# PSUM handed out by single banks and later by pairs, with the second layer's output products in another order

## The chip, the cores and the metric

The kernel runs on one core of one Trainium2 chip. The metric is the device time of one execution in microseconds. TensorE (PE in the views; its weight loads are PEld) multiplies matrices into PSUM, which has eight banks of 512 fp32 columns on 128 partitions. VectorE (DVE) and ScalarE (ACT) read PSUM and work on SBUF, GpSimd (POOL) works on SBUF, and SyncE (SP) issues all transfers.

## What is computed

Causal attention over 32 heads of 576 tokens with a bias from a running sum, and then two dense layers with nonlinearities, 2304 tokens wide, in fp32:

```python
s_pos = np.maximum(s, 0.0)
cum = np.cumsum(s_pos, axis=-1)
bias = -(cum[:, :, :, None] - cum[:, :, None, :])
scores = np.where(causal, -1000000000.0, scores + np.minimum(bias, 0.0))
attn = np.exp(scores - np.max(scores, axis=-1, keepdims=True))
attn = attn / (np.sum(attn, axis=-1, keepdims=True) + 1e-09)
x = (attn @ v)                       # reordered to 2304 x 512
h = x @ w_in;   x = (h - np.tanh(h)) @ w_out          # layer 1, 512 -> 2048 -> 512
h = x @ w2_in;  x = (h * np.clip(h + 3.0, 0.0, 6.0) / 6.0) @ w2_out    # layer 2
```

## The kernel before

**Precision.** A matrix product with fp32 accuracy is made of three products of rounded halves: high by high, low by high, high by low. So nearly every operand exists as a high and a low part. ACT makes the high part by a copy, DVE (or POOL) the low part by a subtraction.

**Order.** The kernel hands its work to a planner (`Plan`, L134). Every piece of work is an `op` with an engine, an assumed duration, what must come before it, the buffers it takes (`Buf`) and a priority. `schedule` (L163) plays the plan through: an engine that is free takes the ready piece with the lowest priority number for which all buffers are free in their `Pool`. The pieces are then written out in the order of their planned starts. On the chip each engine executes its own list in that order and waits on semaphores where data or a buffer is not free yet. What an instruction waits for is found per tile, so a change of the tiles changes waits even where the lists stay equal.

**PSUM.** Four tiles `wide0` to `wide3` of 1024 columns, two banks each (L287). In attention `wide0` as a whole takes the first part of the row maxima. The six halves of the other three are the pool `banks` (L290). After the last row maximum the halves of `wide0` join it (L706). In layer 1 the hidden results come from the halves of `wide0` and `wide1` (`hidp`), the four accumulators from those of `wide2` and `wide3` (`accp`). In layer 2 a product needs two banks; `Pairs` (L96) hands out the first `wide` tile whose two halves are free.

**Attention** (L424 to L662), for each head: `mx` (L500, TensorE) multiplies queries and keys and `rd` (L509, DVE) takes row maxima from PSUM; `st` (L593) makes scores in four chunks, `ex` (L596, ACT) exponentials into `pt`; `pv` (L624) multiplies `pt` with the values into two banks, and ACT copies them out (L647).

**Layer 1** goes over five token blocks (512, 512, 256, 512, 512) and in each over 16 slices of 128 hidden columns (`step_ops`, L833). A step is: hidden matmuls in three parts of four (L842), tanh on ACT (L853), the subtraction on DVE (L857), a copy on ACT into `gg` (L861), the low half on DVE (first three blocks) or POOL (L863), and output matmuls in three parts of four (L873) into the accumulators. Beside it the weights are unpacked and, in `group` (L937), those of layer 2 are prepared into seven pieces for each quarter and stored in DRAM (`wdram`).

**Layer 2** multiplies 2x2 block matrices with seven products instead of eight. For each of three groups of 768 tokens: `prepare` (L1051) loads the inputs and splits seven operands into `op` tiles (`split_tile`, L1045: ACT L1047, DVE L1048; additions L926). `hidden_group` (L1071) makes the seven hidden products for each of four quarters (12 matmuls of 384 columns each, L1091) with copies and additions on ACT and DVE (L1099, L1102). `out_phase` (L1133) makes the seven output products, each over the four quarters (18 matmuls of 256 columns for each quarter, L1164), with their operand splits, and stores the outputs. The products are named by the numbers in `ORDER` (L54); the position in it sets priorities. Products 1, 6, 7 and 4 add up in one pair of banks (`chain`), 5 and 3 in a second, 2 in a third. Product 4 comes after the result of product 7 is added to `p5` (`c22`), since it goes on adding to the same pair. Operands of the output products use the pool `oop`, three buffers before. Every product has its weight piece of 512 KB loaded from `wdram` (`weights`, L1039) into one of the buffers of `piecep`: the two halves of the layer-1 weight slots 4 to 8, ten in all (L1020).

## Time and profile before

| | |
|---|---|
| median of 3 runs | 1008.09 us (1007.0 to 1009.53) |
| the profiled execution | 1012.46 us, span 1010.7 us |
| mean granted TensorE clock in it | 0.996 |
| TensorE busy | 966.9 us, 96% of the span, 5560 matmuls |
| weight loads, DVE, ACT, POOL busy | 840.2, 660.3, 466.2, 160.7 us |

The views are of the one profiled execution; its span runs from the first to the last instruction. The end of a matmul is modelled and overlaps the next one's start, so matmuls are 0.37 us long in the mean where they start every 0.23 us. A wait is named after what ended it.

### The profile page before, as it was taken

The numbers are of one execution on the slowest core, as the hardware profiler recorded it, in microseconds if no ns is written. First come the engines' busy times: TensorE is split into PE (matmuls) and PEld (weight loads), VectorE is DVE, ScalarE is ACT, GpSimd is POOL, SyncE is SP. The second block draws the span as 40 slices with busy tenths as digits, with TensorE's granted clock in tenths as the row PEclk, the third lists the DMA queues.
The fourth block names the chain that finished last, engine by engine and source line by source line (L and its number), as shares of the span: only waits on it lengthen the run. The fifth ranks groups of instructions, "written<-read, shape, count | busy, mean of one in ns | idle before, by whom it ended". The sixth has DMA issues, their size and how long they took to land.

```text
span 1010.7 us, 15024 instructions
## 1 busy us (share of the span) xinstructions
PE 966.9 (96%) x5560; PEld 840.2 (83%) x5560; DVE 660.3 (65%) x1106; ACT 466.2 (46%) x714; POOL 160.7 (16%) x106
## 2 busy tenths in 40 slices
PE   4989989999999999999999999999899998999998
PEld 3667766767777777898888888899899998999998
DVE  7765665746997766677557674365954659455673
ACT  2556655664543444344434434344544445344442
POOL 8243636440000000001223222100000000000000
PEclk9999999999999999999999999999999999999999
DMA  4644857477633654655454763488788886887872
GB/s 118 173 132 119 209 149 194 143 214 253 205 108 108 227 183 160 239 168 189 186 182 142 250 230 135 145 266 268 257 264 281 251 284 228 273 282 251 251 244 82
DMA packets 71816, 203.24 MB, mean 201 GB/s; under 512 B 11778, under 2 KB 20482, under 8 KB 70464
## 3 DMA queue, kind: packets, MB, share of 16 engines
q1 hardware_dynamic: 71744, 202.29, 63.1%
q8 instruction: 44, 0.72, 0.3%
q14 instruction: 28, 0.23, 0.1%
HBM read 151.09 MB, written 44.09 MB: 193 GB/s over the span
## 4 chain that ended last, share of the span: by engine, by line
PE 83%; DVE 9%; ACT 4%; issue 3%; DMA 1%; POOL 0%; DVEq 0%; ACTq 0%; POOLq 0%
PE wide L842 20%; PE wide L873 18%; PE wide L1091 17%; PE wide L1164 11%; PE wide L624 9%; PE wide L593 6%; DVE junk L509 2%; PE wide L500 2%; ACT pt L596 1%; DVE f_w L926 1%; DVE op_W L1048 1%; DVE op_B L1048 1%; DMA xr<-xdram 1%; DMA f_w<-xdram 1%; DVE g L857 0%
## 5 line engine op out<-in xcount | busy, mean ns | idle before, releaser
L842 PE MATMUL wide<-xx,w 128*128 128x512 f32 (+1 forms) x960 | 235.5, 371 | 3.0 <-DVE g L857 2.9
L873 PE MATMUL wide<-gg,w 128*128 128x512 f32 (+1 forms) x960 | 234.7, 369 | 0.4 <-ACT gg L861 0.3
L842 PEld LDWEIGHTS wide<-xx,w 128*128 128x128 f32 x960 | 168.5, 188 | 39.1 <-DVE g L857 8.4
L873 PEld LDWEIGHTS wide<-gg,w 128*128 128x128 f32 x960 | 170.4, 188 | 31.3 <-ACT gg L861 1.2
L509 DVE CUSTOM_DVE_ANT_0 junk<-wide,maskA 128x384 bf16<-128x384 f32 (+4 forms) x160 | 86.8, 542 | 57.2 <-PE wide L500 28.2
L624 PE MATMUL wide<-pt,vf 128*66 128x320 f32 (+4 forms) x448 | 116.0, 373 | 7.2 <-DVE Mt L509 4.5
L853 ACT ACTIVATE g<-wide 128x512 f32<-128x512 f32 (+1 forms) x80 | 44.4, 555 | 135.7 <-PE wide L842 57.1
L863 POOL TENSOR_TENSOR gg<-g,gg 128x512 fp32r<-128x512 f32 x32 | 48.0, 1501 | 358.4 <-ACT gg L861 268.0
L857 DVE TENSOR_TENSOR g<-wide,g 128x512 f32<-128x512 f32 (+1 forms) x80 | 50.7, 634 | 79.4 <-ACT g L853 60.9
L593 PE MATMUL wide<-Q,K 128*128 128x320 f32 (+9 forms) x384 | 94.4, 367 | 5.9 <-ACT pt L596 3.2
L1164 PE MATMUL wide<-w,op_B 128*128 128x256 f32 x702 | 92.5, 284 | 4.7 <-DVE op_B L1048 4.7
L1164 PE MATMUL wide<-w,op_W 128*128 128x256 f32 x702 | 91.9, 284 | 2.2 <-DVE op_W L1048 1.3
L1164 PEld LDWEIGHTS wide<-w,op_B 128*128 128x128 f32 x702 | 87.7, 191 | 6.1 <-DVE op_B L1048 6.1
L1164 PEld LDWEIGHTS wide<-w,op_W 128*128 128x128 f32 x702 | 87.5, 191 | 3.6 <-DVE op_W L1048 2.1
L596 ACT ACTIVATE pt<-wide 128x512 f32<-128x512 f32 (+2 forms) x128 | 62.4, 501 | 60.5 <-PE wide L593 30.5
L593 PEld LDWEIGHTS wide<-Q,K 128*128 128x128 f32 (+1 forms) x384 | 65.2, 198 | 29.8 <-ACT pt L596 10.6
L1091 PE MATMUL wide<-op_w,w 128*128 128x384 f32 x432 | 80.0, 335 | 0.1
L861 ACT ACTIVATE gg<-g 128x512 fp32r<-128x512 f32 (+1 forms) x80 | 47.0, 587 | 64.8 <-DVE g L857 34.0
L1091 PEld LDWEIGHTS wide<-op_w,w 128*128 128x128 f32 x432 | 75.1, 188 | 0.9 <-DVE g L857 0.6
L624 PEld LDWEIGHTS wide<-pt,vf 128*66 128x66 f32 (+1 forms) x448 | 51.7, 141 | 20.9 <-DVE Mt L509 5.8
L500 PE MATMUL wide<-K,Q 66*128 66x384 f32 (+5 forms) x192 | 48.6, 369 | 15.9 <-DMA K<-rb 9.9
L446 POOL TENSOR_TENSOR Q<-tq,Q 64x1152 fp32r<-64x1152 f32 (+1 forms) x17 | 42.4, 2493 | 79.5 <-PE wide L593 36.4
(261 smaller groups left out, 1274.5 us busy)
## 6 DMA issues: line engine op xcount, KB each, us to landing
w<-wdram SPq DMA_DIRECT2D x168, 512.0 KB
wdram<-cv SPq DMA_DIRECT2D x56, 512.0 KB
raw_c<-in_w_dram SPq DMA_DIRECT2D x11, 1024.0 KB
raw_b<-in_w_dram SPq DMA_DIRECT2D x11, 1024.0 KB
raw_a<-in_w_dram SPq DMA_DIRECT2D x12, 512.0 KB
vf<-in_v_dram SPq DMA_DIRECT2D x16, 330.0 KB
rb<-rdram SPq DMA_DIRECT2D x8, 576.0 KB
xdram<-xb SPq DMA_DIRECT2D x16, 288.0 KB
```

What stands on the lines that cost most here:

```text
L500: nc.tensor.matmul(r(b)[0:rr, col + k0 : col + k0 + n], qa[0:66, i * P : i * P + rr], ka[0:66, k0 : k0 + n], start=True, stop=True,)
L509: nc.vector.tensor_tensor_reduce(out=junk[0:rr, 0:w], in0=r(b)[0:rr, col : col + w], in1=maskA[0:rr, m0 : m0 + w], scale=1.0, scalar=-3.0e ...
L593: nc.tensor.matmul(o, w, x, start=(i == 0), stop=(i == len(mms) - 1))
L596: nc.scalar.activation(r(pt), r(b)[:, 0 : CW[c]], AF.Exp, scale=0.125)
L624: nc.tensor.matmul(r(po[bank])[0:DV, oc : oc + n], r(vf)[0:rr, j, hh, :], r(pts[c])[0:rr, col : col + n], start=(j == 0), stop=(bank == 0 ...
L842: nc.tensor.matmul(r(ps)[:, 0:w], wt[:, c, :], x(c)[:, 0:w], start=(part == 0 and c == 0), stop=(part == 2 and c == NCC - 1),)
L857: nc.vector.tensor_sub(x, r(ps)[:, 0:w], x)
L861: gho = plan.op("ACT", vec_us(w, 1.2, 205), lambda: nc.scalar.activation(r(gh)[:, 0:w], r(g)[:, 0:w], AF.Copy), [m, to_gg], [g, gh], base)
L863: glo = plan.op("DVE" if beside else "POOL", vec_us(w, 0.96, 155) if beside else vec_us(w, 0.44, 160), lambda: (nc.vector if beside else n ...
L873: nc.tensor.matmul(r(acc[e])[:, 0:w], a[:, es], bb[:, 0:w], start=f, stop=l)
L1091: nc.tensor.matmul(bank(k)[:, l], w[:, hw, l, kc], r(x)[:, hx, kc], start=(i in (1, 5, 2) and j == 0 and kc == 0), stop=(j == 2 and kc == ...
L1164: nc.tensor.matmul(r(c[k])[0][:, m * 256 : (m + 1) * 256], r(x)[:, hx, l, m * P : (m + 1) * P], w[:, hw, l], start=(i in (1, 5, 2) and q = ...
```

## The change

PSUM is cut into eight tiles of one bank. `bank0` to `bank5` serve attention beside one tile of two banks, `wide`. After the last row maximum `wide` is given back and its place becomes `bank6` and `bank7`. In layer 1 hidden results and accumulators of all blocks but the last take any bank; in the last block hidden results take banks 0, 1, 6 and 7, accumulators 2 to 5. When the last hidden result is read and the blocks before are stored, the first four become the tiles `pair0` and `pair1`, and after the last block's results the others become `pair2` and `pair3`. The class `Pairs` is gone.

For the output products of layer 2, the order of priorities is (1, 5, 2, 6, 3, 7, 4) instead of (1, 5, 6, 3, 7, 2, 4), and their pieces are prepared in that order. Slot 8 of the old weights is no longer cut into two weight pieces but becomes a fourth operand buffer in `oop`; eight pieces are left.

```diff
-ORDER = (1, 5, 6, 3, 7, 2, 4)
+ORDERS = ((1, 5, 6, 3, 7, 2, 4), (1, 5, 2, 6, 3, 7, 4))
...
-    psum = ctx.enter_context(tc.tile_pool(name="psum", bufs=1, space=PS))
-    wides = [psum.tile([P, 1024], F32, name=f"wide{i}") for i in range(4)]
-    pairs = [(w, w[:, 0:512], w[:, 512:1024]) for w in wides]
-    widep = Pool([wides[0]])
-    banks = Pool([half for pair in pairs[1:] for half in pair[1:]], keep=2)
-    hidp, accp = (Part(banks, [half for pair in two for half in pair[1:]]) for two in (pairs[0:2], pairs[2:4]))
-    pairp = Pairs(banks, pairs)
+    stacks = {k: ctx.enter_context(ExitStack()) for k in ("left", "wide", "right")}
+
+    def bank_tiles(key, names, n=512):
+        side = "right" if key == "right" else "left"
+        p = stacks[key].enter_context(tc.tile_pool(name=f"psum_{names[0]}", bufs=1, space=PS, side=side))
+        return [p.tile([P, n], F32, name=x) for x in names]
+
+    hids, accs = bank_tiles("left", ["bank0", "bank1"]), bank_tiles("right", [f"bank{i}" for i in range(2, 6)])
+    widep = Pool(bank_tiles("wide", ["wide"], 1024))
+    banks = Pool(hids + accs, keep=2)
+    hidp, accp = Part(banks, hids + ["bank6", "bank7"]), Part(banks, accs)
+    pairp = Pool([])
...
-        acc = [Buf(accp, greedy=True) for _ in range(NCC)]
+        final = bi == len(BLOCKS) - 1
+        acc = [Buf(accp if final else banks, greedy=True) for _ in range(NCC)]
...
+            hid_done = hid_done + [hs[3]] if fc else [hs[3]]
...
+    plan.op("V", 0.0, all_left, hid_done + sum((evs[b2] for b2 in range(len(BLOCKS) - 1)), []), prio=0, name="pair0", hook=lambda: pairp.free.extend(["pair0", "pair1"]))
+    plan.op("V", 0.0, again("right", ["pair2", "pair3"], 1024), hid_done + evs[len(BLOCKS) - 1], prio=0, name="pair2", hook=lambda: pairp.free.extend(["pair2", "pair3"]))
...
-    for fc in range(4, 9):
+    for fc in range(4, 8):
...
-    for fc in (9, 15):
+    for fc in (8, 9, 15):
...
-                to, x, d = split_tile(g[b], oop, after, base + 40 * ORDER.index(i) + 10 * q + 1)
+                to, x, d = split_tile(g[b], oop, after, base + 40 * ORDERS[1].index(i) + 10 * q + 1)
...
-        store("s1", 0, 0, add("s1", 3, [s1, p2], base + 240))
+        store("s1", 0, 0, add("s1", 3, [s1, p2], base + 120))
```

TensorE in attention, rows of before around the stall that the views show at 74.19 us (its row is the one of `pt1_0_104`). Names carry the tile and a running number; `[waits ...]` names the engine whose semaphore is waited for.

```order
L500 MATMUL wide3_68<-K1_1_90,Q1_1_89 128x256 [waits Activation_49]
L500 MATMUL wide3_68<-K1_1_90,Q1_1_89 128x128
L624 MATMUL wide1_66<-pt0_0_102,vf0_99 66x256
L500 MATMUL wide0_65<-K1_2_92,Q1_2_91 128x384 [waits DMAHW2_49,DVE_49]
L500 MATMUL wide0_65<-K1_2_92,Q1_2_91 64x128
L500 MATMUL wide0_65<-K1_2_92,Q1_2_91 64x448
L624 MATMUL wide3_68<-pt1_0_104,vf0_99 66x320 [waits DVE_49]
L593 MATMUL wide2_67<-Q2_1_97,K2_1_98 128x256 [waits Activation_49]
```

And the same place in the changed kernel:

```order
L478 MATMUL bank4_72<-K1_1_99,Q1_1_98 128x256 [waits Activation_49]
L478 MATMUL bank4_72<-K1_1_99,Q1_1_98 128x128
L602 MATMUL bank0_65<-pt0_0_111,vf0_108 66x256 [waits Activation_49]
L478 MATMUL wide_77<-K1_2_101,Q1_2_100 128x384 [waits DMAHW2_49,DVE_49]
L478 MATMUL wide_77<-K1_2_101,Q1_2_100 64x128
L478 MATMUL wide_77<-K1_2_101,Q1_2_100 64x448
L602 MATMUL bank5_73<-pt1_0_113,vf0_108 66x320 [waits Activation_49]
L571 MATMUL bank3_71<-Q2_1_106,K2_1_107 128x256 [waits Activation_49]
```

The order is the same; the matmul of `pt1` writes a tile that the row maxima of `K1_1` do not use, and waits for ACT where it waited for DVE.

TensorE in the second block of layer 1, before, at 368.9 to 373 us: hidden parts (L842, out of `xx`) of slices 9 between output parts (L873).

```order
L842 MATMUL wide0_65<-xx_1772,w8_1876 128x512 x4
L873 MATMUL wide2_67<-gg_1862,w6_1874 128x512 [waits Activation_49]
L873 MATMUL wide3_68<-gg_1862,w6_1874 128x512 x2
L873 MATMUL wide2_67<-gg_1862,w6_1874 128x512
L842 MATMUL wide0_65<-xx_1772,w9_1877 128x512 x4
L873 MATMUL wide2_67<-gg_1862,w6_1874 128x512
L873 MATMUL wide3_68<-gg_1862,w6_1874 128x512 x2
L873 MATMUL wide2_67<-gg_1862,w6_1874 128x512
L842 MATMUL wide0_65<-xx_1772,w9_1877 128x512 [waits DVE_49]
L842 MATMUL wide0_65<-xx_1772,w9_1877 128x512 x3
```

And in the changed kernel:

```order
L827 MATMUL bank3_71<-xx_1787,w8_1891 128x512 x4
L858 MATMUL bank6_1683<-gg_1877,w6_1889 128x512
L858 MATMUL bank2_70<-gg_1877,w6_1889 128x512
L858 MATMUL bank5_73<-gg_1877,w6_1889 128x512
L858 MATMUL bank4_72<-gg_1877,w6_1889 128x512
L827 MATMUL bank7_1684<-xx_1787,w9_1892 128x512 x4
L858 MATMUL bank6_1683<-gg_1877,w6_1889 128x512 [waits DVE_49]
L858 MATMUL bank2_70<-gg_1877,w6_1889 128x512
L858 MATMUL bank5_73<-gg_1877,w6_1889 128x512
L858 MATMUL bank4_72<-gg_1877,w6_1889 128x512
L827 MATMUL bank7_1684<-xx_1787,w9_1892 128x512 x4
```

The hidden parts of slices 8 and 9 now go to tiles of their own and wait for nothing; they also stand one part later against the output parts.

TensorE at the start of the first output stage of layer 2, before (695 us on; L1091 are hidden products, L1164 output products; `wide0` is product 5, the `wide1` rows beside it are product 1, and behind the three further rows of `wide0` product 6 follows in `wide1`):

```order
L1164 MATMUL wide1_66<-w7_1875,op_W15_4791 128x256 x18
L1091 MATMUL wide2_67<-op_F_4537,w6_1874 128x384 x12
L1164 MATMUL wide0_65<-w8_1876,op_B_4792 128x256 x18
L1164 MATMUL wide1_66<-w8_1876,op_W15_4791 128x256 x18
L1164 MATMUL wide1_66<-w6_1874,op_B_4792 128x256 x18
L1164 MATMUL wide1_66<-w4_82,op_W15_4791 128x256 x18
L1164 MATMUL wide0_65<-w5_83,op_B_4792 128x256 x18
L1164 MATMUL wide0_65<-w7_1875,op_W15_4791 128x256 x18
L1164 MATMUL wide0_65<-w5_83,op_B_4792 128x256 x18
L1164 MATMUL wide1_66<-w4_82,op_W15_4791 128x256 x18
L1164 MATMUL wide1_66<-w7_1875,op_B_4792 128x256 x18
```

And in the changed kernel (`pair3` is product 1, `pair0` product 5, `pair2` product 2, and the last row product 6):

```order
L1157 MATMUL pair3_4813<-w6_1889,op_w9_4505 128x256 x18
L1084 MATMUL pair1_4639<-op_F_4508,w4_91 128x384 x12
L1157 MATMUL pair0_4638<-w4_91,op_W15_4747 128x256 x18
L1157 MATMUL pair3_4813<-w7_1890,op_w9_4505 128x256 x18
L1157 MATMUL pair2_4812<-w4_91,op_B_4748 128x256 x18
L1157 MATMUL pair3_4813<-w5_92,op_W15_4747 128x256 x18
L1157 MATMUL pair3_4813<-w7_1890,op_w9_4505 128x256 x18
L1157 MATMUL pair0_4638<-w5_92,op_B_4748 128x256 x18
L1157 MATMUL pair0_4638<-w6_1889,op_W15_4747 128x256 x18
L1157 MATMUL pair0_4638<-w6_1889,op_w9_4505 128x256 x18
L1157 MATMUL pair2_4812<-w4_91,op_B_4748 128x256 x18
L1157 MATMUL pair2_4812<-w7_1890,op_W15_4747 128x256 x18
```

Product 2 now stands among products 1 and 5 and ahead of product 6. Three operand tiles go round in both lists; the fourth, `op_w8`, is used by one product near the stage's end. At the very end of the program the four products of number 4 now follow those of number 7, where those of number 2 stood between.

## Rows read from the trace of the kernel before

**Rows 1.** The page, part 1: busy us, share of the span, instructions.

```profile
PE 966.9 (96%) x5560; PEld 840.2 (83%) x5560; DVE 660.3 (65%) x1106; ACT 466.2 (46%) x714; POOL 160.7 (16%) x106
```

**Rows 2.** Stages: length, busy us and count by engine, granted clock, DMA share, GB/s.

```profile
25.00:235.00 210.00, 196.05 (x1091) 142.98 (x1089) 134.26 (x419) 127.57 (x241) 90.89 (x40) 0.98 0.61 164
235.00:410.00 175.00, 171.68 (x740) 136.73 (x739) 135.85 (x189) 76.06 (x110) 0.10 (x1) 1.00 0.54 182
...
695.00:735.00 40.00, 36.77 (x288) 35.54 (x287) 35.45 (x41) 22.02 (x28) 0.00 (x0) 1.00 0.75 256
735.00:819.00 84.00, 84.00 (x559) 84.00 (x558) 43.02 (x47) 33.86 (x40) 0.00 (x0) 1.00 0.84 268
819.00:859.00 40.00, 36.46 (x287) 35.24 (x286) 35.16 (x41) 22.17 (x28) 0.00 (x0) 1.00 0.77 255
```

**Rows 3.** Waits of TensorE in attention, 25 to 235: total us, times, longest.

```profile
PE wide L624 <- DVE Mt L509: 4.5, 6, 1.4
PE wide L593 <- ACT pt L596: 2.7, 3, 1.1
PE wide L624 <- ACT pt L596: 2.3, 5, 0.8
PE wide L593 <- DVE Mt L509: 1.4, 1, 1.4
PE wide L500 <- DVE Mt L509: 1.2, 2, 0.8
...
PE wide L624 <- ACT stage L647: 0.4, 2, 0.2
```

**Rows 4.** Timeline of TensorE: start, us, instruction, count, idle before and releaser.

```profile
74.19 1.33 PE L624 MATMUL wide<-pt,vf 128*66 128x320 f32 x2 [1.36 <-DVE Mt L509]
...
76.02 2.17 PE L624 MATMUL wide<-pt,vf 64*66 64x64 f32 x6
...
84.63 1.23 PE L624 MATMUL wide<-pt,vf 64*66 64x64 f32 x6 [0.55 <-DVE Mt L509]
```

**Rows 5.** Stages as in rows 2; the figure after POOL is the granted clock.

```profile
75.00:80.00 5.00, 5.00 (x18) 3.69 (x18) 2.44 (x8) 0.38 (x1) 0.00 (x0) 0.50 0.45 151
```

**Rows 6.** Timeline of all engines in layer 1, 366 to 373.5.

```profile
368.90 1.07 PE L842 MATMUL wide<-xx,w 128*128 128x512 f32 x4
...
369.81 1.07 PE L873 MATMUL wide<-gg,w 128*128 128x512 f32 x4
...
370.00 0.60 ACT L853 ACTIVATE g<-wide 128x512 f32<-128x512 f32 x1 [0.81 <-PE wide L842]
370.63 0.69 DVE L857 TENSOR_TENSOR g<-wide,g 128x512 f32<-128x512 f32 x1 [0.83 <-ACT g L853]
...
371.38 1.19 PE L842 MATMUL wide<-xx,w 128*128 128x512 f32 x4 [0.51 <-DVE g L857]
```

**Rows 7.** Timeline of TensorE in an undisturbed stretch of layer 1.

```profile
479.67 1.07 PE L842 MATMUL wide<-xx,w 128*128 128x512 f32 x4
...
486.02 1.07 PE L873 MATMUL wide<-gg,w 128*128 128x512 f32 x4
```

**Rows 8.** The page, part 5: busy us, mean ns of one, idle before.

```profile
L863 POOL TENSOR_TENSOR gg<-g,gg 128x512 fp32r<-128x512 f32 x32 | 48.0, 1501 | 358.4 <-ACT gg L861 268.0
```

**Rows 9.** Timeline of DVE in the first output stage of layer 2.

```profile
711.95 0.95 DVE L1048 TENSOR_TENSOR op_raw_c<-f_w,op_raw_c 128x768 fp32r<-128x768 f32 x1
...
713.69 0.95 DVE L1048 TENSOR_TENSOR op_B<-f_C,op_B 128x768 fp32r<-128x768 f32 x1
```

**Rows 10.** The chain that ended last: start, us, what, count.

```profile
658.32 37.46 PE wide L1091 x216
...
700.44 6.00 DMA f_w<-xdram
...
965.73 40.59 PE wide L1164 x336
```

**Rows 11.** Timeline of all engines at the end of the program.

```profile
1002.04 0.95 DVE L1183 TENSOR_TENSOR f_A<-f_A,wide 128x768 f32<-128x768 f32 x1 [0.69 <-PE wide L1164]
...
1004.00 2.32 PE L1164 MATMUL wide<-w,op_B 128*128 128x256 f32 x18
...
1006.35 0.81 ACT L1180 ACTIVATE f_w<-wide 128x768 f32<-128x768 f32 x1 [5.99 <-PE wide L1164]
```

More of the change, by code (lines that the diff above doesn't have):

```diff
@@ L93, in append @@
         self.whole.free.append(t)
-class Pairs:
-    def __init__(self, whole, pairs):
-        self.whole, self.pairs, self.keep = whole, pairs, 0
-    @property
-    def free(self):
-        return self
-    def ready(self):
-        have = {id(t) for t in self.whole.free}
-        return [p for p in self.pairs if id(p[1]) in have and id(p[2]) in have]
-    def __len__(self):
-        return len(self.ready())
-    def pop(self, _):
-        pair = self.ready()[0]
-        for half in pair[1:]:
-            self.whole.free.pop(next(i for i, t in enumerate(self.whole.free) if t is half))
-        return pair
-    def append(self, pair):
-        self.whole.free.extend(pair[1:])
 class Buf:
@@ L703, with again, fn @@
             batch(p // NCC)
-    plan.op("V", 0.0, lambda: None, rd_done, prio=0, hook=lambda: banks.free.extend(pairs[0][1:]))
+    def again(key, names, n):
+        def fn():
+            stacks[key].close()
+            late.update(zip(names, bank_tiles(key, names, n)))
+        return fn
+    plan.op("V", 0.0, again("wide", ["bank6", "bank7"], 512), rd_done, prio=0, hook=lambda: banks.free.extend(["bank6", "bank7"]))
     def close_attention():
@@ L950, in use @@
             cv, y = Buf(cvp), ys[b[0]][0]
-            k = base + 1 + ORDER.index(i)
+            k = base + 1 + ORDERS[m].index(i)
             def part(h):
@@ L957, in use @@
             d = plan.op("DVE", vec_us(512, 0.96, 155), lambda: nc.vector.tensor_sub(part(1), view(b), f32(part(0))), [c], [y, cv], k, port=True)
-            puts[m, q, i] = plan.dma(lambda: move(wdram[m, q, ORDER.index(i)], r(cv)), 512, [d], [cv], 5999)
+            puts[m, q, i] = plan.dma(lambda: move(wdram[m, q, ORDERS[m].index(i)], r(cv)), 512, [d], [cv], 5999)
             return [c, d]
@@ L974 @@
         split = oh + ol
-        acc = [Buf(accp, greedy=True) for _ in range(NCC)]
+        final = bi == len(BLOCKS) - 1
+        acc = [Buf(accp if final else banks, greedy=True) for _ in range(NCC)]
         prev = []
         for fc in range(NFC):
-            hs, o2 = step_ops(bi, fc, oh, ol, prev, acc)
+            hs, o2 = step_ops(bi, fc, oh, ol, prev, acc, hidp if final else banks)
             prev = [o2]
             wfree[fc, 0], wfree[fc, 1] = [hs[2]], [o2]
+            hid_done = hid_done + [hs[3]] if fc else [hs[3]]
         hreads = [([hs[1]], [hs[2]])] * NCC
@@ L986, with all_left @@
                     group(m, quarter)
+    def all_left():
+        stacks["wide"].close()
+        again("left", ["pair0", "pair1"], 1024)()
     xop, oop, fp, piecep = (Pool([]) for _ in range(4))
@@ L1042, in weights @@
         return pc, plan.dma(
-            lambda: move(r(pc), wdram[m, q, ORDER.index(i)]), 320, loaded[: 7 * 8], [pc], prio, name=f"pc{m}_{q}_{i}")
+            lambda: move(r(pc), wdram[m, q, ORDERS[m].index(i)]), 320, loaded[: 7 * 8], [pc], prio, name=f"pc{m}_{q}_{i}")
     def split_tile(src, pool, after, prio):
@@ L1063, in use @@
         def use(i, b, after):
-            to, c, d = split_tile(bufs[b], xop, after, prio + 0.1 * ORDER.index(i))
+            to, c, d = split_tile(bufs[b], xop, after, prio + 0.1 * ORDERS[0].index(i))
             tiles[i] = (to, [c, d])
@@ L1078, in bank @@
         def bank(k):
-            return r(c[k])[0].rearrange("p (l n) -> p l n", l=2)[:, :, 0:HT]
+            return r(c[k]).rearrange("p (l n) -> p l n", l=2)[:, :, 0:HT]
         def product(i, after):
-            prio = base + 10 * ORDER.index(i)
+            prio = base + 10 * ORDERS[0].index(i)
             pc, ld = weights(0, q, i, prio)
@@ L1173, in bank @@
         def bank(k):
-            return r(c[k])[0][:, 0 : 2 * HT]
+            return r(c[k])[:, 0 : 2 * HT]
         def flat(name):
@@ L1196, in out_phase @@
         p6 = product(6, [s1])
-        u2 = copy("u2", 1, p6, base + 120)
+        u2 = copy("u2", 1, p6, base + 160)
         p3 = product(3, [k5])
-        store("u2", 0, 1, add("u2", 2, [u2, p3], base + 160))
+        store("u2", 0, 1, add("u2", 2, [u2, p3], base + 200))
         p7 = product(7, [u2])
-        c22 = add("p5", 1, [k5, p7], base + 200)
+        c22 = add("p5", 1, [k5, p7], base + 220)
         store("p5", 1, 1, c22)
         p2 = product(2, [])
-        store("s1", 0, 0, add("s1", 3, [s1, p2], base + 240))
+        store("s1", 0, 0, add("s1", 3, [s1, p2], base + 120))
         p4 = product(4, [c22])
```

12 lines of the change are left out of this document (6 added, 6 removed).

## The prediction, made before the run

> **What bounds the kernel now.** First read the busy times [rows 1]: TensorE is busy for 966.9 of 1010.7 us and no other engine for more than 660, so the time is TensorE's work plus its idle time. Then the stages [rows 2], where TensorE's busy time is held against the length of each: attention (25 to 235 us) leaves 13.95 us idle, the first two token blocks of layer 1 (235 to 410) leave 3.3, two short stretches of layer 2 (695 to 735 and 819 to 859) leave 3.2 and 3.5, and 735 to 819 leaves nothing. An idle figure is too small, because the end of a matmul is modelled and overlaps the next one. What is lost is better read from the pitch. Undisturbed, 28 matmuls of 512 columns start within 486.02 - 479.67 = 6.35 us [rows 7], 0.227 us each; a product of 384 columns takes 37.46/216 = 0.173 and one of 256 takes 40.59/336 = 0.121 [rows 10]. So 235 to 410 holds 740 x 0.227 = 168 us of work in 175: **7 us lost**. 695 to 735 holds 288 matmuls, 16 of them of 384 columns: 272 x 0.121 + 16 x 0.173 = 35.6 of 40, **4.4 us lost**, and 819 to 859 the same.
>
> Third, what ended those waits. In attention [rows 3] TensorE waits for DVE in front of L624 (4.5 us), for ACT in front of L593 (2.7) and L624 (2.3), for DVE in front of L593 (1.4) and L500 (1.2), and 0.4 for ACT's L647. L624 multiplies exponentials of ACT with values from a DMA, and L593 multiplies queries and keys: neither reads anything that DVE's L509 wrote. So these waits are for PSUM to be read out. The order shows whose PSUM: at the stall of 74.19 [rows 4] the L624 matmul writes one half of wide3 and waits for DVE, which reads the other half.
>
> **Single banks in attention.** Removed: the first 1409 instructions of TensorE, up to the first steps of layer 1's second block, all keep their place, and so do those of the other engines beside them; only what they wait for changes. At 74.19 the matmul writes bank5 and waits for ACT instead. By the same reading the waits of [rows 3] go, except those for data: L624 for ACT's exponentials may stay (2.3). That leaves 4.5 + 2.7 + 1.4 + 1.2 + 0.4 = 10.2 us, and each of some 14 waits hides about 0.15 us more under the modelled end (at 371.38 [rows 6] the view shows 0.51 idle, but the start came 371.38 - 369.81 - 4 x 0.227 = 0.66 late): 2.1 us. Together 12.3. Below, only the waits that cannot be for data are sure to go, 4.5; above, all 12.5 of [rows 3], the hidden 3, and some 5 for ACT and DVE, which drop such waits too and so deliver earlier: 20. I take 12, nearest to the rows themselves. ACT and DVE are busy 128 and 134 of the 210 us, so neither bounds a stage that is 12 us shorter. One more: after the idle 1.36 us at 74.19 the granted clock is 0.50 from 75 to 80 us [rows 5], 1.2 instead of 2.4 GHz, and six matmuls take 2.17 us that at 84.63 take 1.23 [rows 4]. Those some 3 us go too if the idle time brought the clock down, but this execution is 4.4 us above the median of the runs and they may be part of that. I leave them out of the sum.
>
> **Single banks in layer 1.** At 368.90 to 371.38 [rows 6] the tanh of a step starts when its last hidden matmul ends (370.00, 0.60), the subtraction follows (370.63, 0.69), and only then may the next hidden step begin in the other half of the same tile. With eight banks it begins in a bank that was read four steps ago, and the wait is gone. Of the 7 us some 1 stays: waits for gg, which is data. Gain 6, between 3 and 7. The order also moves the hidden steps later: hidden work runs 7 to 10 parts ahead of the output work from the third block on, where it ran 12 to 14. From a step's last hidden matmul to its first output part there are still four hidden and four output parts, 8 x 4 x 0.227 = 7.3 us, against 0.60 + 0.69 + a copy of ACT of about 0.6; the low half, 1.50 us on POOL [rows 8], is wanted 3.6 us after that. I cost it at nothing; without this cover it is the last rival.
>
> **From banks to pairs.** Pair0 waits for the last hidden subtraction. Eight output matmuls stand between them, 1.8 us against 0.60 + 0.69 + 0.2: nothing, and 1.5 us once if that cover fails, with the rest of the last block's output work queued behind it. Until the last block is read out there are two pairs, as before; nothing. The pairs are taken in turn where the first free one was taken; nothing. The second matrix's pieces are made in another order in layer 1, with the same instructions and bytes, on ACT and DVE, busy 76 and 136 of 175 us there: nothing.
>
> **The order of the output products.** Both stretches of 4.4 us are DVE's. From 711.95 it starts an instruction every 0.87 us ([rows 9]: 713.69 - 711.95 = 2 x 0.87) and TensorE waits for its op tiles. By the old order DVE has 30 instructions between the splits that the stage's third and fourteenth output product need, 26.1 us, for 11 products of 18 x 0.121 = 2.17 us, 23.9. The rest of the 4.4 is DVE's own idle time in front of the first splits, which wait for a free operand buffer. Now product 2, whose operand is a plain quarter without an addition, comes third. Between the splits for the third and the twelfth product DVE has 20 instructions for nine products, 17.4 us against 19.5. So it keeps up, with little to spare. I leave 0.5 us in each stretch: gain 2 x 3.9 = 7.8, between 4 and 8.8. The fourth operand buffer does not add to it: by the order one product's split, of the last product, fills it before the stage begins and holds it to the end, so three go round as before.
>
> The price stands at the end. Products 7 and 4 add up in one PSUM pair, and 4 must wait until DVE has added 7's result to p5. Product 2 used to run between them. In the first two groups of 768 tokens a layer-2 hidden product now covers it; in the last nothing does. Product end to engine start is small (the last product ends at 1004.00 + 2.32, ACT starts at 1006.35 [rows 11]), an addition takes 0.95 (1002.04), so 0.95 + 0.2 = 1.2 us, between 1.0 and 2. Behind it queue four output products, the last copy and the last store.
>
> **Two weight pieces fewer.** Bytes and loads are the same: 168 of 512 KB. A piece is fetched as soon as the product that used its buffer is done, and by the order most now have seven products of lead, 14 us, where they had nine. Five loads have only two output products, 4.3 us. The trace shows 6.00 us from issue to landing for a load behind others of its kind (700.44 [rows 10]), so each may be 0 to 1.7 us late. A weight load is seldom behind three others: I take 0.7 in all, between 0 and 8.5. The loads of the next group's inputs stand on SP where they stood, behind the fifth weight load of the stage.
>
> **The sum.** -12 - 6 - 7.8 + 1.2 + 0.7 = -23.9 us. The profiled execution took 1012.5 with a span of 1010.7, so it would be 988.6, or 985 with the clock; the median of the runs is 1008.1, so the forecast is **984**.
>
> **Rivals.** (1) The waits move on. In attention a freed TensorE meets the waits for data behind, and only the 4.5 us in front of L624 go: 7.5 us less gain, 992. For it: L624's wait for ACT is data, and no order was changed to fill what is freed. Against it: ACT and DVE are 60% busy there and lose such waits as well.
> (2) More goes than I count: attention gives the 20 of its upper bound, layer 1 its 7, and the outputs the full 8.8: 1008.1 - 35.8 + 1.9 = 974 and, if the median runs too had the slow clock, 971.
> (3) More PSUM brings nothing. Then only the output products count: 1008.1 - 7.8 + 1.9 = 1002. For it would be a TensorE that is fed late by DMA anyway; against it, the DVE waits above, while from 25 us on no wait of [rows 3] is for a DMA. The Trainium skill has a result of this kind, which speaks against the change: in "TensorE: Matmul & The Clock Gate", section "HAM oscillation — how this bites in real kernels", double-buffering PSUM gave a kernel no further gain (126.6 to 125.5 us). No stage of this trace agrees with it, as here the named waits are PSUM's.
> (4) Slower: the shortened lead in layer 1. If in the last two blocks the low half on POOL no longer lands in time, each of their 32 steps loses up to the 1.50 us of that instruction: 48 - 24 = +24, 1032. It decides from 24/32 = 0.75 us per step on. For it: there is one g buffer, and POOL's read frees it. Against it: 7.3 us of cover against some 2 of ACT and DVE.
>
> **How the numbers follow.** Chances: the forecast 0.62 (its own range 976 to 991), waits that move on 0.17, more gain 0.08, no gain from PSUM 0.07, slower 0.06. The range must leave out no more than 2 in 10: 969 to 1000 takes in the first three and leaves out the last two and a little of the rest. About 0.3%, 3 us, is what a measurement of this kernel can tell from no change. Rival 3 spreads from 998 to 1008, so I give 0.04 of it to the same; with the others, faster 0.90, same 0.04, slower 0.06.
>
> **What would show it.** In attention no wait of L624 or L593's successors for DVE's L509, and busy time of TensorE within 3 us of that stage's length, some 198 us; no 0.50 clock at 75 us. In layer 1 no hidden matmul that waits for the subtraction. In layer 2 the two stretches without 1 us waits for op tiles, one wait of 1.2 us for a DVE addition some 13 us before the end, and perhaps waits for w tiles. Wrong would be: attention as long as before, waits of the second layer's products for DMA beyond 3 us in all, or steps of the last two blocks that wait for gg.

## The result and the profile after

The changed kernel takes **973.43 us** (median of 4 runs, 972.57 to 977.29); the kernel before took 1007.55 in the same comparison (1006.56 to 1009.53). The ratio is 0.9666 (95% interval 0.9636 to 0.9696): 34 us are gone, where 24 were forecast. 984 was missed by 10.6 us on the fast side, the range from 969 to 1000 holds the time, and what came is closest to rival 2 (974 or 971).

The profiled execution took 972.57 us with a span of 970.8, 39.9 less than that of before. Of these 39.9, 4.9 are due to the earlier execution lying above its median and 0.9 to the later one lying below its own; 34.1 are left for the medians. Two executions among the experiments below, one of 1080.18 us (halves) and one of 3299.55 us (product 7 ahead of 3), stand far from all the others and are left out of medians and ratios.

The page of the kernel after, part 1, against [rows 1]:

```profile
PE 947.8 (98%) x5560; PEld 839.5 (86%) x5560; DVE 665.1 (69%) x1106; ACT 467.4 (48%) x714; POOL 159.9 (16%) x106
```

Stages of the kernel after, columns as in [rows 2]: attention, the last two blocks of layer 1, the first output stage of layer 2:

```profile
25.00:210.00 185.00, 184.59 (x1088) 140.70 (x1087) 136.40 (x419) 128.79 (x241) 91.46 (x40) 1.00 0.69 186
383.00:602.00 219.00, 219.00 (x1144) 188.98 (x1143) 143.84 (x197) 91.04 (x156) 45.78 (x32) 1.00 0.52 182
669.00:690.00 21.00, 21.00 (x177) 21.00 (x176) 17.84 (x22) 13.40 (x17) 0.00 (x0) 1.00 0.89 319
```

TensorE is idle for 0.4 us of attention, where [rows 2] leave 14, and the granted clock of its row is 1.00 where before has 0.98. All its waits in the whole kernel (waiter, line, what ended the wait: total us, times, longest):

```profile
PE wide L478 <- DMA K<-rb: 9.9, 1, 9.9
PE wide L478 <- DMA K<-cdram: 3.1, 1, 3.1
PE wide L478 <- DVE Mt L487: 1.4, 1, 1.4
PE pair L1157 <- DVE f_W L1176: 1.0, 1, 1.0
PE pair L1084 <- DMA w<-wdram: 0.8, 2, 0.6
PE pair L1157 <- DMA w<-wdram: 0.7, 1, 0.7
PE pair L1084 <- DVE f_w L1104: 0.6, 1, 0.6
PE bank L858 <- ACT gg L846: 0.3, 1, 0.3
PE bank L602 <- ACT pt L574: 0.3, 1, 0.3
```

The first three are the start of the kernel and stand in both. Of the waits of [rows 3] one of 0.3 us is left; the waits for operand tiles in layer 2 are gone; new are 1.5 us for weight pieces and 1.0 for an addition (`f_W`, L1176).

Since both kernels have 5560 matmuls, and the same first 1409 TensorE instructions, the stages can be measured between equal matmuls:

| from, to | before | after | difference | forecast |
|---|---|---|---|---|
| first matmul to the first of layer 1 | 9.93 to 234.82 | 9.93 to 209.76 | -25.1 | -12 |
| to the 3301st matmul (layer 1 is done) | to 684.51 | to 651.67 | -7.8 | -6 |
| to the last matmul (the rest of layer 2) | to 1006.04 | to 966.14 | -7.1 | -5.9 |

So layer 1 and layer 2 came out close to the forecast, and the miss is attention.

### The profile page after: what moved, and what is told of

Same layout as the page of the kernel before. It is cut to its first block, busy times and chain, and to the rows that moved or that the text cites. A ratio compares the mean times of both kernels' runs of the same rounds, so it can differ in the third digit from the quotient of the medians.

```text
span 970.8 us, 14991 instructions
## 1 busy us (share of the span) xinstructions
PE 947.8 (98%) x5560; PEld 839.5 (86%) x5560; DVE 665.1 (69%) x1106; ACT 467.4 (48%) x714; POOL 159.9 (16%) x106
## 4 chain that ended last, share of the span: by engine, by line
PE 94%; DVE 3%; DMA 2%; ACT 1%; issue 0%; DVEq 0%; ACTq 0%
PE bank L827 20%; PE bank L858 20%; PE pair L1084 18%; PE pair L1157 17%; PE bank L602 10%; PE bank L571 7%; PE wide L478 2%; DMA w<-wdram 1%; PE bank L478 1%; DVE junk L487 1%; ACT w L775 0%; DVE f_w L1104 0%; DMA K<-rb 0%; DVE rb L369 0%; DVE w L776 0%
## 5 line engine op out<-in xcount | busy, mean ns | idle before, releaser
L858 PE MATMUL bank<-gg,w 128*128 128x512 f32 (+1 forms) x960 | 234.3, 368 | 0.5 <-ACT gg L846 0.3
L827 PE MATMUL bank<-xx,w 128*128 128x512 f32 (+1 forms) x960 | 233.3, 368 | 0.0
L858 PEld LDWEIGHTS bank<-gg,w 128*128 128x128 f32 x960 | 170.1, 189 | 30.9 <-ACT gg L846 1.3
L827 PEld LDWEIGHTS bank<-xx,w 128*128 128x128 f32 x960 | 170.5, 188 | 30.3
L602 PE MATMUL bank<-pt,vf 128*66 128x320 f32 (+4 forms) x448 | 113.0, 366 | 0.3 <-ACT pt L574 0.3
L842 DVE TENSOR_TENSOR g<-bank,g 128x512 f32<-128x512 f32 (+1 forms) x80 | 50.8, 635 | 70.0 <-ACT g L838 69.4
L571 PE MATMUL bank<-Q,K 128*128 128x320 f32 (+9 forms) x384 | 93.9, 367 | 0.0
L1084 PE MATMUL pair<-op_w,w 128*128 128x384 f32 x432 | 79.9, 335 | 1.4 <-DMA w<-wdram 0.8
L1084 PEld LDWEIGHTS pair<-op_w,w 128*128 128x128 f32 x432 | 75.0, 188 | 2.4 <-DMA w<-wdram 1.2
L1157 PE MATMUL pair<-w,op_w 128*128 128x256 f32 x558 | 72.0, 283 | 1.0 <-DVE f_W L1176 1.0
L1157 PEld LDWEIGHTS pair<-w,op_w 128*128 128x128 f32 x558 | 69.5, 192 | 1.2 <-DVE f_W L1176 1.2
L602 PEld LDWEIGHTS bank<-pt,vf 128*66 128x66 f32 (+1 forms) x448 | 51.8, 139 | 11.7 <-issue 1.6
```

The source lines that it names most:

```text
L571: nc.tensor.matmul(o, w, x, start=(i == 0), stop=(i == len(mms) - 1))
L602: nc.tensor.matmul(r(po[bank])[0:DV, oc : oc + n], r(vf)[0:rr, j, hh, :], r(pts[c])[0:rr, col : col + n], start=(j == 0), stop=(bank == 0 ...
L827: nc.tensor.matmul(r(ps)[:, 0:w], wt[:, c, :], x(c)[:, 0:w], start=(part == 0 and c == 0), stop=(part == 2 and c == NCC - 1),)
L842: nc.vector.tensor_sub(x, r(ps)[:, 0:w], x)
L858: nc.tensor.matmul(r(acc[e])[:, 0:w], a[:, es], bb[:, 0:w], start=f, stop=l)
L1084: nc.tensor.matmul(bank(k)[:, l], w[:, hw, l, kc], r(x)[:, hx, kc], start=(i in (1, 5, 2) and j == 0 and kc == 0), stop=(j == 2 and kc == ...
```

## Experiments

Where a run is compared with the changed kernel, the ratio to the kernel before is used, since the four runs of each group below share runs of the kernel before on their chip (medians 1011.09, 1011.51 and 1010.72). "Lost" and "gained" by stage are between the same matmuls as above, against the first profile of the changed kernel.

### Which waits were they: halves again, and each side alone

**The same list with halves.** Every bank is cut as one half of a two-bank tile; the instructions and their order are the same on all engines, only what they wait for differs.

```diff
-        return [p.tile([P, n], F32, name=x) for x in names]
+        return [p.tile([P, n], F32, name=x) for x in names] if n == 1024 else [w[:, i : i + 512] for w in [p.tile([P, 1024], F32, name=x) for x in names[::2]] for i in (0, 512)]
```

> The changed kernel with every single bank cut as one half of a two-bank tile again (banks 0 and 1, 2 and 3, 4 and 5, 6 and 7); the instructions and their order are the same on all engines, only waits come back. Theory (waits for the other half of a tile are the whole gain of attention and layer 1): attention is about 25 us longer in the profile than the changed kernel's 200 us, some 22 of them in waits of TensorE and 3 in a stretch at the 1.2 GHz clock if that comes back with the waits; layer 1 is 6 to 8 longer; in all 1001 to 1007 us. Rival A (the freer hand-out of banks moved layer 1's steps apart, and that is its gain): attention as in the theory, layer 1 as short as in the changed kernel, 993 to 998. Rival B (the slow clock was an accident of the one profiled execution): no stretch at 0.50, 998 to 1003.

Measured: 1019.05 us, ratio 1.0076 (1.0056 to 1.0096), above all three expectations, because of layer 1. In attention 23.2 us are lost, and the waits of [rows 3] are back almost to the tenth:

```profile
PE bank L602 <- DVE Mt L487: 4.5, 6, 1.4
PE bank L571 <- ACT pt L574: 2.8, 4, 1.1
PE bank L602 <- ACT pt L574: 2.4, 5, 0.8
PE bank L571 <- DVE Mt L487: 1.4, 1, 1.4
```

That settles attention: nearly all of its gain is the waits for the other half of a tile. Layer 1 lost 17.2 us, more than the 7.8 that the change gained there. The changed kernel lets hidden results and accumulators take any bank; with halves that is worse than the fixed halves of before, so this hand-out depends on single banks. Which pairs of users cost the 9.4 us more was not taken apart, and single banks under the old hand-out were not run, so how much of the 7.8 each of the two makes stays open. Layer 2 lost 6.4; 4.5 of that is waits for weight pieces (6.0 where the first profile has 1.5) and about 1.7 a low clock (below): the waits for weight pieces come without this edit too (the changed kernel's second profile, below).

**Each side alone.** Single banks, and dependencies that bring back one kind of wait: a function around the instructions adds, for a matmul into a bank, the last readers of the neighbouring bank (kind "pe"), or, for an instruction that reads a bank, the last matmul into the neighbour (kind "reader").

```diff
+            if name == "matmul":
...
+                    if kind == "pe":
+                        for x in read.pop(n ^ 1, {}).values():
+                            wait(ins, x)
+                    wrote[n] = ins
...
+                if kind == "reader" and n ^ 1 in wrote:
+                    wait(ins, wrote[n ^ 1])
+                read.setdefault(n, {})[id(eng)] = ins
```

> The changed kernel, same order, single banks; a matmul that writes a bank waits, as before, for the readers of the neighbouring bank (0 and 1, 2 and 3, 4 and 5, 6 and 7), but ACT and DVE don't wait for matmuls of the neighbour. Theory (TensorE's own waits are the 12 us that I summed for attention, the rest of the 25 comes by ACT and DVE, which delivered later): 12 to 15 us longer in attention and 5 to 7 in layer 1, 990 to 996 us. Rival (ACT and DVE have slack, and nearly all was lost at TensorE's own waits, which I read too small): 20 to 25 longer in attention, 999 to 1006, the same as with both kinds of wait.

> The changed kernel, same order, single banks; ACT and DVE, when they read a bank, wait also for the last matmul that was written into the neighbouring bank, and TensorE's waits stay as in the changed kernel. Theory (about half of attention's gain came by ACT and DVE): 8 to 12 us longer, 981 to 986 us. Rival (they have slack): 0 to 3 us longer, 973 to 977.

Measured: TensorE's side 991.24 us, ratio 0.9802 (0.9783 to 0.9822); the readers' side 979.42, ratio 0.9686 (0.9668 to 0.9704). In attention TensorE's side loses 11.9 us, the readers' side 0.6, and both together (halves) 23.2. In layer 1 it is 3.5, 1.5 and 17.2.

Of the 11.9, 2.0 do not come from the edit. Near 30 us ten matmuls that wait for nothing take 3.87 us with TensorE's side alone and 2.09 in the changed kernel's first profile (first and second row):

```profile
30.53 3.87 PE L1289 MATMUL bank<-pt,vf 64*66 64x64 f32 x10
```

```profile
29.54 2.09 PE L602 MATMUL bank<-pt,vf 64*66 64x64 f32 x10
```

The changed kernel loses the same 2.0 us at the same matmuls in its own second profile (below), without any edit. So TensorE's side costs 9.9 us, less than the 12 to 15 expected, and in the views it shows 3.8 us of waits in attention, where [rows 3] have more than three times as much:

```profile
PE bank L1289 <- DVE Mt L1289: 3.0, 5, 0.7
PE bank L1289 <- ACT pt L1289: 0.8, 3, 0.3
```

The theory was near for TensorE's own waits, the rival right for ACT and DVE alone, and both missed the point: **the two kinds together cost far more than their sum**. A run with both functions at once was not made; "together" is the run with halves. The rest of the readers' run is mainly its weight loads, 5.9 us of waits in its profile.

The traces show how. ACT's waits in attention with halves (for L602's product, which an exponential does not read; in the changed kernel this row does not exist):

```profile
ACT pt L574 <- PE bank L602: 19.2, 19, 2.1
```

One place with halves (start, us, instruction, count, idle before and releaser):

```profile
147.70 1.03 PE L602 MATMUL bank<-pt,vf 128*66 128x192 f32 x4
...
148.76 0.38 ACT L625 ACTIVATE stage<-bank 66x256 f32<-66x256 f32 x1 [0.77 <-PE bank L602]
...
149.05 0.69 ACT L574 ACTIVATE pt<-bank 128x256 f32<-128x256 f32 x2
...
149.47 0.90 PE L571 MATMUL bank<-Q,K 128*128 128x64 f32 x4 [0.74 <-ACT pt L574]
```

And the same matmuls with TensorE's side alone (helper lines read L1289):

```profile
141.05 0.38 ACT L1289 ACTIVATE stage<-bank 66x256 f32<-66x256 f32 x1
...
141.33 0.69 ACT L1289 ACTIVATE pt<-bank 128x256 f32<-128x256 f32 x2
141.37 1.03 PE L1289 MATMUL bank<-pt,vf 128*66 128x192 f32 x4
...
141.99 1.03 PE L1289 MATMUL bank<-Q,K 128*128 128x64 f32 x4
```

By the lists the copy (`stage`) reads bank 0, the four matmuls write bank 1, the exponential reads bank 3 and the scores write bank 2. With halves the copy of the finished bank 0 starts when the matmuls into bank 1 have ended, not before; the exponential queued behind it on ACT starts 0.3 later, and the scores wait 0.74 us for it. With TensorE's side alone the copy runs ahead of these matmuls, the exponential beside them, and the scores start at once. In these runs a late reader cost next to nothing while TensorE did not wait for it (0.6 us), and a TensorE that waits for readers lost 9.9 us while they were on time; where both wait, each makes the other later.

**The kernel before, a second time.**

> The kernel before, unchanged, profiled a second time. If the stretch at a granted clock of 0.50 near 75 us belongs to this order of work, it comes back at the same place and the mean clock is 0.996 again; if it was an accident of the first profiled execution, there is none, the mean clock is 1.0, the span is about 3 us shorter than 1010.7 and attention ends near 231.5 instead of 234.8 us.

Measured: one time, 1013.78 us, span 1012.0. Attention is 25.3 us longer than in the changed kernel, where the first profile has 25.1; 2.0 of it are the slow matmuls near 30 us again. A low clock is there again, at another place and shorter (columns as in [rows 2]):

```profile
205.00:210.00 5.00, 3.85 (x18) 2.68 (x18) 2.60 (x11) 1.80 (x4) 1.22 (x1) 0.81 0.86 199
210.00:215.00 5.00, 5.00 (x28) 3.80 (x26) 2.01 (x3) 2.75 (x6) 2.63 (x1) 0.85 1.07 214
```

It is neither bound to 75 us nor an accident of one execution. With halves the clock fell in attention and in layer 2:

```profile
60.00:65.00 5.00, 5.00 (x24) 3.60 (x24) 1.93 (x6) 1.46 (x4) 0.00 (x0) 0.74 0.42 112
...
760.00:765.00 5.00, 5.00 (x30) 5.00 (x29) 0.24 (x1) 1.41 (x2) 0.00 (x0) 0.76 0.32 104
```

In all three the low stretch lies at or right behind an idle time of TensorE of 1.1 to 1.8 us. In attention it costs 3.1 us in the first profile of before, 1.5 in the second and 1.7 with halves; in the changed kernel it is absent. Without the low clock and the difference near 30 us (-0.1, 2.0 and -0.4), attention loses about the same in all three: 22.1, 21.8 and 21.9 us.

### Layer 2: order, operand buffers, weight pieces

**The changed kernel again**, on the chip of the next three.

> The changed kernel, unchanged, on the same chip as the next three. On the chip of the last runs two kernels with the same layer 2 waited 5.9 and 6.0 us for weight pieces, where its own profile showed 1.5. If that belongs to the chip or the execution, and not to what those kernels changed, its waits for weight pieces are again over 3 us in all, and its time is 974 to 979 us; if it came from the added waits, they are 1 to 2 us and the time is 972 to 975.

Measured: 978.39 us (973.22 to 980.46), ratio 0.9661 (0.9638 to 0.9685): the ratio is that of the first comparison. The waits for weight pieces are 5.1 us now, so they belong to the chip or the execution. They stand at four loads that are issued two products ahead of their use; the prediction counted five such loads (three of TensorE's waits, then two loads from the chain of waits, with the time from issue to landing):

```profile
674.42 1.82 PE L1157 MATMUL pair<-w,op_B 128*128 128x256 f32 x13 [0.96 <-DMA w<-wdram]
...
720.00 1.31 PE L1084 MATMUL pair<-op_w,w 128*128 128x384 f32 x6 [2.13 <-DMA w<-wdram]
...
841.18 1.14 PE L1084 MATMUL pair<-op_w,w 128*128 128x384 f32 x5 [1.60 <-DMA w<-wdram]
```

```profile
713.59 6.37 DMA w<-wdram
...
835.29 5.84 DMA w<-wdram
```

A load of 6.37 us with 4.3 us of lead is 2.1 late, which is the wait at 720.00. The slow matmuls near 30 us cost this profile another 2.0. So the term of the weight pieces differs between chips or executions, from 1.5 to 6.0 us in the profiles of kernels that share it.

**Three operand buffers, ten pieces.**

```diff
-    for fc in range(4, 8):
+    for fc in range(4, 9):
...
-    for fc in (8, 9, 15):
+    for fc in (9, 15):
```

> The changed kernel with ten weight pieces and three operand buffers, as before. By the order one operand buffer is held by product 4's first split from early on, so here two go round, where three do in the changed kernel. Theory (as I predicted: the fourth buffer adds nothing, DVE's pace decides): no wait of output products for operand tiles over 1 us in all, waits for weight pieces gone or under 1 us, so 0 to 4 us faster than the changed kernel on this chip. Rival (with two buffers going round a split cannot start until the product before the last is done): waits for operand tiles of 3 to 10 us in the three output stages, 2 to 8 us slower.

Measured: 982.76 us, ratio 0.9716 (0.9696 to 0.9735): about 5 us slower than the changed kernel, the rival. The waits for operand tiles are about those of before, whose largest row comes first:

```profile
PE wide L1164 <- DVE op_B L1048: 4.7, 7, 1.1
```

```profile
PE pair L1157 <- DVE op_B L1041: 4.8, 6, 1.1
...
PE pair L1157 <- DVE op_w L1041: 0.6, 2, 0.5
```

Layer 2 from the 3301st matmul on takes 324.2 us; before it took 321.5, in the changed kernel 314.5. With the new order alone nothing of the 7 us is left. In the lists one buffer is held by an early split in before and here, so two go round; the changed kernel has one more, and three go round. (The section on the change says that three go round in both lists; its rows of before show two, `op_W15` and `op_B`, those of the changed kernel three.)

**All three go round.** As the last, with product 4's first split planned behind product 3, so that no buffer is held.

```diff
-        p3 = product(3, [k5])
+        p3 = product(3, [k5]); p3.next.append(ops[4, 0][1][0]); ops[4, 0][1][0].left += 1
```

> As ten pieces and three operand buffers, but product 4's splits are ordered behind product 3, so that no buffer is held and three go round. If the number that goes round decides, no waits for operand tiles come (under 1 us in all), and with ten pieces the waits for weight pieces are under 2 us: 0 to 4 us faster than the changed kernel. If the early split of product 4 was itself of use (DVE has less to do later), waits for operand tiles of 1 to 3 us stand late in each output stage, and it is 2 us faster to 4 slower.

Measured: 974.52 us, ratio 0.9632 (0.9614 to 0.9651). Waits for weight pieces are 0.5 us, waits for operand tiles 3.6 (1.8, 1.1 and 0.7). Beside ten pieces with a held buffer it gains about 0.8%: the number that goes round decides. The remaining 3.6 speak for the second expectation: the early split was of some use.

**The old order with three buffers going round.** The changed kernel with the old order and the old priorities; product 2's first split behind product 3, so that only one of four buffers is held.

```diff
-ORDERS = ((1, 5, 6, 3, 7, 2, 4), (1, 5, 2, 6, 3, 7, 4))
+ORDERS = ((1, 5, 6, 3, 7, 2, 4), (1, 5, 6, 3, 7, 2, 4))
...
-        p3 = product(3, [k5])
+        p3 = product(3, [k5]); p3.next.append(ops[2, 0][1][0]); ops[2, 0][1][0].left += 1
```

> The changed kernel with the old order of output products (1, 5, 6, 3, 7, 2, 4) and eight pieces; product 2's splits are ordered behind product 3, so that only one of the four operand buffers is held and three go round, as in the changed kernel. Theory (the buffers that go round made the 8 us of the output stages, and the order of the products nothing): waits for operand tiles under 1.5 us in all three stages together, and no wait for the addition of product 7; ratio 0.963 to 0.967. Rival (the order is needed as well, as the prediction has it: by the old order DVE has 26.1 us of work for 23.9 of TensorE's): waits for operand tiles of 1.5 to 2.5 us in each of the three stages, 4 to 8 in all, ratio 0.968 to 0.973.

Measured: 972.55 us, ratio 0.9622 (0.9607 to 0.9638), not slower than the changed kernel. Waits for operand tiles:

```profile
PE pair L1157 <- DVE op_w L1041: 1.1, 1, 1.1
PE pair L1157 <- DVE op_W L1041: 1.0, 1, 1.0
...
PE pair L1157 <- ACT op_w L1040: 0.3, 1, 0.3
```

2.4 us in all lie between the two expectations: so much the new order saves in waits for operand tiles. But the old order pays nothing for product 4 (1.05 us in the changed kernel), and no wait for a weight piece stands in its profile (1.5). Between equal matmuls layer 2 takes 314.1 us here, 314.5 in the changed kernel: the buffer that goes round makes the gain, and no net gain of the new order is shown.

**The PSUM part alone**: old order and priorities, three operand buffers, ten pieces (the edits of the last two without the late split).

> The changed kernel with the old order of output products, ten weight pieces and three operand buffers: the PSUM part of the change alone. If the parts add up, attention and layer 1 are as long as in the changed kernel (25 and 8 us shorter than before in the profiles), and layer 2 is as long as in the kernel before (321.5 us from its first products to the last, against 314.5): ratio 0.972 to 0.974. If layer 2 gains from the pairs too (they are taken in turn, and free of the halves' bookkeeping), it is under 318 us and the ratio under 0.970.

Measured: 980.14 us, ratio 0.9696 (0.9682 to 0.9711), a little below the 0.972 to 0.974 expected. Attention and layer 1 are within 0.1 us of the changed kernel's, layer 2 takes 322.2 us as before (321.5). The parts add up, and PSUM alone makes 3.0% of the 3.3 to 3.4% that the whole change brings.

**Loads in the order of use.** The loads' priorities follow TensorE's order, and the next group's first hidden products are planned behind product 7; every load then has at least seven products of lead.

```diff
-            pc, ld = weights(0, q, i, prio)
+            pc, ld = weights(0, q, i, prio if q or not sb else base - 265 + 10 * ORDERS[0].index(i))
...
-                pc, ld = weights(1, q, i, prio)
+                pc, ld = weights(1, q, i, {(5, 0): base + 5, (2, 0): base + 15}.get((i, q), prio))
```

> The changed kernel, in which the loads of weight pieces stand on SP's queue in the order in which TensorE uses them, and the first hidden products of the next group of tokens come behind product 7; every load then has seven products of lead, where five had two. Theory (the waits for weight pieces, 5.0 us in the second profile of the changed kernel and at the five places that the prediction named, come from the lead alone): no such wait is left (under 0.5 us in all), ratio to the kernel before 0.961 to 0.963, where the changed kernel has 0.966. The wait for the addition of product 7 stands in the last group only. Rival (the loads are late because the DMA engines are busy with other loads there): the waits stay over 2 us in all, at these or at later places, ratio 0.964 to 0.967.

Measured: 972.61 us, ratio 0.9627 (0.9614 to 0.9640). No wait for a weight piece is left in the profile; in layer 2 TensorE waits once for the addition of product 7, as expected, and once 0.6 us for a hidden result (L1104), as in the changed kernel. The theory holds, by the trace; the ratio's interval touches that of the changed kernel.

**Product 7 ahead of 3 in the last group.**

```diff
-        base = 2500 + 1000 * sb
+        base, turns = 2500 + 1000 * sb, ORDERS[1] if sb + 1 < NSB else (1, 5, 2, 6, 7, 3, 4)
```

> The changed kernel, in whose last group of tokens product 7 comes ahead of product 3, so that the addition of 7's result runs beside 3's four matmul groups and 4 need not wait. Theory (the 1.05 us in front of the first matmul of product 4 is that addition and nothing else waits there): the wait is gone and the time 0.5 to 1.2 us shorter than the changed kernel's. Rival (DVE, which must make 7's operands four products earlier, is late in their place): waits for operand tiles of 1 us or more in the last 40 us, no gain or 0 to 2 us slower.

Measured: 975.47 us, ratio 0.9648 (0.9633 to 0.9663), no difference that can be told. The wait did not go, it moved in front of product 7:

```profile
944.57 1.69 PE L1157 MATMUL pair<-w,op_W 128*128 128x256 f32 x12 [0.90 <-ACT xr L1173]
```

7 goes on adding to the pair of 6, whose result ACT must have copied first. Neither expectation saw it: 1, 6, 7 and 4 all share a pair, and each needs another product between.

**Both, with that order mended**: the loads as above, and (1, 5, 6, 2, 7, 3, 4) in the last group.

> The changed kernel with the loads in order of use, as in the run with the longer lead, and in the last group of tokens the order (1, 5, 6, 2, 7, 3, 4), in which no two neighbouring products add up in the same pair: 6, 2, 7, 3, 4. If the wait of product 4 for the addition of 7's result and its copy (0.9 us in front of 7, when 7 was put right behind 6) come from that neighbourhood alone, neither is there, and the time is 0.5 to 1.2 us shorter than with the loads alone: ratio 0.960 to 0.962. If DVE is late with 6's operands, which now come one product earlier, waits for operand tiles of 1 us or more stand in the last stage, and there is no gain.

Measured: **970.58 us**, ratio 0.9604 (0.9591 to 0.9617), the fastest kernel here; its interval lies below both of the changed kernel's, which begin at 0.9636 and 0.9638 and were taken on other chips. The last output stage has no wait. It is 2.0 us below the kernel with the loads alone, more than the 1.05 us of that wait. Between equal matmuls layer 2 takes 311.8 us against 312.6, 0.9 less, which is about that wait; the intervals of the two kernels overlap, and the second microsecond is not shown.

## Why the prediction was right, and where it was not

- **What bounds it, and which waits go: right.** Attention's waits were for the other half of a two-bank tile: the same list with halves brings back 23.2 of 25.1 us.
- **Attention, -12, measured -25.1: the term that failed.** It summed the idle rows of TensorE's own waits. The failing step is "some 5 for ACT and DVE", a figure without a row, which stood in the upper bound and not in the sum: the waits of ACT and DVE alone cost 0.6, but together with TensorE's some 11 more. That TensorE's side alone costs 9.9, near the 12, is luck: its run has 3.8 us of idle rows, not the 10.2 that were summed, so most of those rows were already the work of both sides. By the same step the 2.3 us of "data" (L624 behind ACT) was left standing; 0.3 is left of it, since ACT was late for the same reason. Matched matmul by matmul, the 25.1 are 13.9 us of idle time, 7.1 that the modelled ends hide at 34 waits (0.21 each, where I took 0.15 at 14), 3.1 of clock and 1.0 of small change. Layer 1 I had read by its pitch and came out close; attention I read by its idle rows, and these show half.
- **The clock, left out: wrong by 1.5 to 3.1 us in a profile.** It fell in all three profiles of kernels with these stalls, so it was no accident of the first.
- **Layer 1, -6, measured -7.8: near**, just beyond the upper bound of 7. With halves under the new hand-out it is a loss of 9.4, so with this hand-out the gain needs single banks.
- **The last rival (the shortened lead): did not come.** One wait for gg of 0.3 us is left, and 383 to 602 us is full.
- **Banks to pairs, nothing: right**; no wait stands there.
- **Output products, -7.8: the size was near by luck, the reason wrong.** In the first profile 7.1 us net, with 1.0 and 1.5 paid, are 9.6, beyond the upper bound of 8.8. But I wrote that the fourth buffer adds nothing since "three go round as before". In before two went round. The buffer makes the gain; the order saves 2.4 us of waits and pays about as much for product 4 and the weight pieces. DVE's steady pace of 0.87 us [rows 9] was no proof that DVE bounds the stage: among those instructions are splits for the next group (`op_raw_c` in [rows 9] is one), which DVE takes up while it has no buffer for the urgent ones.
- **Product 4 behind 7, +1.2: right**, 1.05, at the place named:

```profile
956.51 0.95 DVE L1176 TENSOR_TENSOR f_W<-f_W,pair 128x768 f32<-128x768 f32 x1 [0.68 <-PE pair L1157]
...
957.52 0.74 PE L1157 MATMUL pair<-w,op_w 128*128 128x256 f32 x4 [1.05 <-DVE f_W L1176]
```

- **Weight pieces, +0.7: right in place, small in size.** 1.5 us in the first profile, 5.1 in the second, at loads with the lead of 4.3 us that it counted, and inside the bounds of 0 to 8.5. But the second is beyond the 3 us that the prediction named as a sign of being wrong, and one load came 2.1 us late where its bound was 1.7. Loads in order of use remove the term.
- **Rival 3** (no gain from PSUM), which the Trainium skill's result in "TensorE: Matmul & The Clock Gate", section "HAM oscillation — how this bites in real kernels", stood for, is refuted for this kernel: PSUM alone gives 0.9696. The Trainium skill's advice in "Perfetto Trace Analysis", section "Matmuls", is to rotate independent matmul groups through different banks. These runs agree, with an addition: with halves the groups use the same banks in the same order and lose 23.2 us in attention, so the banks must also be separate in what the program waits for.

## What to carry to other kernels

In such a program a wait belongs to a tile, not to the bytes that are used: where two users share one, look for it on both sides, at the writer that waits for readers and at the readers that wait for the writer, because here they cost far more together than the sum of each. Measure what a stage loses by its pitch, or between equal instructions; idle rows showed half of it. Of a pool count the buffers that go round, not those that exist, and let loads be issued in the order in which their data is used.

## What the runs showed of the hardware

From 35 us on and before the kernel's end, the granted clock fell from 2.4 to 1.2 GHz in the three profiles with two-bank tiles for all of attention and in none of the eleven others, at or just behind idle times of TensorE of 1.1 to 1.8 us, and not at the same place in two executions of one kernel (74 and 208 us). An idle time alone does not decide it: behind the 2.13 us at 720 us in the second profile of the changed kernel the clock does not fall.

In five of the fourteen profiles the same matmuls between 29 and 34 us take 2.0 us longer, with no wait. In these five the trace's record of the clock begins at 33.4 us or later, with the full clock; in the other nine it begins at 29.5 us or earlier. Before its beginning the views print 1.00 without a reading, so small differences between two profiles are better compared from there on.

Loads of the same 512 KB pieces took 4.5 to 4.9 us on the chain of the changed kernel's first profile and 4.6 to 6.4 in its second, with no difference in the program; what makes that difference stays open.
